# Pooled attention and an affine MLP: two parameter rows made by one product, bias rows written by ScalarE, the mix's rests in one piece

## The chip, the cores and the metric

One core of a Trainium2 chip. The metric is the device time of one execution in microseconds (us). PE is TensorE, PEld its weight loads, DVE VectorE, ACT ScalarE, POOL GpSimd, SP SyncE.

## The reference, cut to what matters

```python
B, H, S, D = 8, 8, 576, 64                       # attention over keys and values averaged by 8 rows
scores = scale * np.matmul(q, k_p.transpose(0, 1, 3, 2))
attn = softmax(scores); x = attn @ v_p           # x: (8, 576, 512)
a1  = alpha1 * x + beta1
tok = np.einsum('ts,bsd->btd', w_tok, a1)        # the "mix" over the 576 tokens
u   = x + lam * tok
a2  = alpha2 * u + beta2
out = u + lam * (np.maximum(a2 @ w_ch1, 0.0) @ w_ch2)
```

The kernel folds lambda into the mix's operand: it needs the row lambda alpha1 broadcast to 128 partitions, and the row lambda beta1 as one extra row of the operand, once for each of its two operand buffers. A "rest" below is the part of an operand that holds the last 64 of the 576 tokens, which four tiles of 128 leave over.

## The kernel before

The opening of the program, in program order for each engine:

```python
vecs = const.tile([65, 3, DM], FP, ...)          # lambda, alpha1, beta1; rows 0 and 64
ones_row = const.tile([1, P], FP, ...)
nc.vector.memset(ones_row, 1.0)
warm = const.tile([P, DM], BF, ...)              # filled by four memsets, used by nothing
...
nc.scalar.dma_start(out=vecs[0:65:64, 0], in_=moe_lam.unsqueeze(0).to_broadcast((2, DM)))
nc.scalar.dma_start(out=vecs[0:1, 1], in_=moe_alpha1.unsqueeze(0))
nc.scalar.dma_start(out=vecs[0:65:64, 2], in_=moe_beta1.unsqueeze(0).to_broadcast((2, DM)))
load_qk(0, 0)                                    # bulk loads on SyncE's queue
load_rem(0)
...
nc.vector.tensor_tensor(out=vecs[0:1, 1], in0=vecs[0:1, 1], in1=vecs[0:1, 0], op=ALU.mult)

def broadcast(i):                                # PE: a row to 128 partitions
    ps = psB.tile([P, DM], FP, tag="ch", bufs=2, name="ps_bc")
    nc.tensor.matmul(out=ps, lhsT=ones_row, rhs=vecs[0:1, i])
    return ps

def row_of_xs(i, eng):                           # lambda beta1, a product on one partition
    p0 = 64 - 64 * i
    eng.tensor_tensor(out=xs_pool[i][p0:p0 + 1, 4, :], in0=vecs[p0:p0 + 1, 2],
                      in1=vecs[p0:p0 + 1, 0], op=ALU.mult)
...
row_of_xs(0, nc.gpsimd)
fill_mix()                                       # GpSimd memsets
ps_lam = broadcast(0)
nc.scalar.copy(out=lam_bc, in_=ps_lam)
ps_lamal = broadcast(1)
nc.scalar.copy(out=lamal_bc, in_=ps_lamal)
cast_q(0, 0, nc.vector.tensor_copy)              # queries to bf16
att_F(0, 0)                                      # PE turns the queries
sum_k(0, 0, nc.vector)                           # pooled keys
fill_E()                                         # 12 VectorE memsets
cast_rem(0, nc.gpsimd)                           # the last 64 tokens' queries and keys
...
att_K(0, 0, nc.vector.tensor_copy, nc.scalar.copy)
...
# first batch of the MLP, among 16 first-product groups:
todo.append((13.0, lambda: row_of_xs(1, nc.gpsimd)))
```

The softmax here doesn't subtract the row's maximum and nothing guards it: scores larger than these inputs give would overflow.

## Time and profile before

| | before |
|---|---|
| median of 3 runs | 368.66 us (367.91 to 369.07) |
| span of the profiled run | 366.2 us |
| busy PE, DVE, ACT, POOL | 97%, 58%, 59%, 35% |
| first exponential (ACT) starts | 11.33 us |
| first mix matmul starts | 24.59 us |
| second product (PE, the output matmuls) starts | 50.47 us |
| from there to the end | 315.72 us |

The span falls into an opening up to the first mix matmul, the first batch up to the second product, and the rest, in which PE is the bound.

### The profile page before, as it was taken

What the parts mean: (1) busy time and instruction counts of PE and PEld (TensorE: products, weight loads), DVE (VectorE), ACT (ScalarE), POOL (GpSimd) and SP (SyncE); (2) the same over time, 40 slices, a digit from 0 to 9 for tenths busy, and PEclk for the clock granted to TensorE, in tenths of its full rate; (3) what the DMA queues carried; (4) which work ended last, traced back from release to release, by engine and by line L of the source; (5) the groups of instructions that cost most, each with busy time, mean ns of one, the idle gap of its engine ahead of it and who ended that gap; (6) DMA issues with size and microseconds to landing.
All of it is one profiled execution on the core that took longest, in us unless ns stands there. A gap on an engine that the chain in (4) does not pass through costs nothing.

```text
span 366.2 us, 6166 instructions
## 1 busy us (share of the span) xinstructions
PE 353.7 (97%) x2340; PEld 192.9 (53%) x2340; DVE 212.9 (58%) x431; ACT 216.1 (59%) x425; POOL 126.4 (35%) x181
## 2 busy tenths in 40 slices
PE   5799999999999999999999999999999999999995
PEld 2367655455545554555455554555455545544543
DVE  7774635883785268724864387627862787543011
ACT  3866993379627960798169924895279615803800
POOL 8856913081509140543245130905090500000000
PEclk9989999999999999999999999999999999999999
DMA  7999994039014910182108311470100002002012
GB/s 249 269 228 319 248 289 128 29 127 345 31 39 147 291 28 33 57 310 79 59 36 307 104 44 44 159 259 29 59 29 2 30 30 58 2 29 86 2 45 71
DMA packets 19552, 43.28 MB, mean 118 GB/s; under 512 B 2169, under 2 KB 4541, under 8 KB 19522
## 3 DMA queue, kind: packets, MB, share of 16 engines
q1 hardware_dynamic: 17496, 37.89, 30.4%
q0 software_dynamic: 1856, 4.86, 7.0%
q8 instruction: 18, 0.29, 0.3%
q10 hardware_dynamic: 170, 0.14, 0.2%
q14 instruction: 12, 0.10, 0.1%
HBM read 38.30 MB, written 9.44 MB: 130 GB/s over the span
## 4 chain that ended last, share of the span: by engine, by line
PE 88%; ACT 6%; DVE 2%; DMA 1%; POOL 1%; issue 0%; ACTq 0%; POOLq 0%
PE ps_ch L587 33%; PE ps_h L564 32%; PE ps_tok L517 9%; PE ps_sc L454 4%; PE ps_av L471 2%; PE ps_uT L548 2%; ACT Hj L569 2%; PE ps_q L370 2%; DMA vecs<-in_moe_beta_dram 1%; PE ps_tok L533 1%; ACT ET L456 1%; ACT qT L374 1%; PE ps_av L474 1%; ACT wtT L292 0%; ACT vp L445 0%
## 5 line engine op out<-in xcount | busy, mean ns | idle before, releaser
L564 PE MATMUL ps_h<-u_fm,w 128*128 128x512 bf16 (+1 forms) x592 | 134.7, 373 | 0.7 <-ACT u_fm L550 0.4
L587 PE MATMUL ps_ch<-w,Hj 128*128 128x512 bf16 x512 | 127.2, 379 | 0.0
L569 ACT ACTIVATE Hj<-ps_h,bias_cols 128x512 bf16<-128x512 f32 x144 | 97.1, 691 | 33.9 <-PE ps_h L564 33.4
L564 PEld LDWEIGHTS <-w 128*128 128x128 bf16 x592 | 63.9, 114 | 48.6 <-issue 0.9
L587 PEld LDWEIGHTS <-Hj 128*128 128x128 bf16 x592 | 55.5, 98 | 49.4 <-issue 0.7
L550 ACT COPY u_fm<-ps_uT 128x512 bf16<-128x512 bf16 x36 | 21.1, 588 | 70.1 <-PE ps_uT L548 70.0
L485 POOL TENSOR_TENSOR xs<-x_tm,lamal_bc 128x512 bf16<-128x512 f32 x24 | 30.5, 1270 | 82.2 <-DVE x_tm L478 81.9
L456 ACT ACTIVATE ET<-ps_sc 128x288 f16<-128x288 f32 (+1 forms) x128 | 51.5, 489 | 10.6 <-PE ps_sc L454 10.3
L594 DVE TENSOR_TENSOR u_sb<-u_sb,ps_ch 128x512 f32<-128x512 f32 (+1 forms) x37 | 24.9, 672 | 24.9 <-PE ps_ch L587 23.8
L517 PE MATMUL ps_tok<-xs,wtT 128*128 128x512 bf16 (+1 forms) x160 | 39.3, 379 | 0.0
L409 DVE CAST kpT<-ps_kp 64x288 bf16<-64x288 f32 x30 | 13.6, 455 | 43.5 <-PE ps_kp L405 43.3
L593 DVE TENSOR_TENSOR ps_ch<-lam_bc,ps_ch 128x512 f32<-128x512 f32 x32 | 22.2, 693 | 25.5 <-PE ps_ch L587 25.4
L478 DVE TENSOR_TENSOR x_tm<-ps_av,rec 128x320 f32<-128x320 f32 x64 | 31.5, 492 | 2.8
L476 DVE RECIPROCAL rec<-ps_av 128x5 f32<-128x5 f32 x64 | 12.3, 193 | 35.2 <-PE ps_av L474 35.2
L138 POOL TENSOR_TENSOR qk_raw<-qk_raw 128x512 f32<-128x512 f32 (+1 forms) x28 | 30.1, 1076 | 1.1
L454 PE MATMUL ps_sc<-qT,kpT 128*128 128x288 bf16 (+1 forms) x128 | 29.0, 300 | 1.0 <-DVE kpT L409 0.5
L519 DVE TENSOR_TENSOR u_sb<-x_tm,ps_tok 128x512 f32<-128x512 f32 x32 | 21.9, 685 | 10.0 <-PE ps_tok L517 9.8
L694 POOL COPY ticks<-ticks 1x1 f32<-1x1 f32 x6 | 1.1, 178 | 70.5 <-DVE ticks L690 70.5
L517 PEld LDWEIGHTS <-wtT 128*128 128x128 bf16 (+1 forms) x160 | 15.1, 98 | 18.7 <-DVE xs L485 1.9
L471 PEld LDWEIGHTS <-ET 72*128 72x128 f16 (+1 forms) x256 | 16.8, 101 | 14.7 <-DVE vp L429 0.7
L417 DVE TENSOR_TENSOR v_u<-v_u 128x512 f32<-128x512 f32 (+1 forms) x30 | 22.2, 741 | 0.8
L520 DVE TENSOR_TENSOR u_bf<-u_sb,al_bc 128x512 bf16<-128x512 f32 x31 | 21.8, 704 | 1.1
(117 smaller groups left out, 335.7 us busy)
## 6 DMA issues: line engine op xcount, KB each, us to landing
qk_raw<-in_q_dram SPq DMA_DIRECT2D x16, 512.0 KB, 5.1
qk_raw<-in_k_dram SPq DMA_DIRECT2D x16, 512.0 KB, 7.5
v_u<-in_v_dram SPq DMA_DIRECT2D x32, 256.0 KB, 8.0
out_dram<-u_sb SPq DMA_DIRECT2D x32, 256.0 KB, 2.3
w<-in_moe_w_ch_dram POOLq DMA_DIRECT2D x2, 1024.0 KB, 12.9
w<-in_moe_w_ch_dram POOLq DMA_DIRECT2D x4, 512.0 KB, 10.8
rem_raw<-in_q_dram SPq DMA_DIRECT2D x8, 128.0 KB, 8.9
rem_raw<-in_k_dram SPq DMA_DIRECT2D x8, 128.0 KB, 4.7
```

Of the source, the lines that this page charges most:

```text
L138: eng.tensor_tensor(out=t[:, :, 0:n], in0=t[:, :, 0:n], in1=t[:, :, n:2 * n], op=ALU.add)
L417: eng.tensor_tensor(out=t[:, :, 0:n], in0=t[:, :, 0:n], in1=t[:, :, n:2 * n], op=ALU.add)
L454: nc.tensor.matmul(out=ps_sc[0:n, 0:288], lhsT=kpT_pool[u][:, j, r, 72 * hh:72 * hh + n], rhs=st["qT"][u][:, h % 4, :])
L456: nc.scalar.activation(out=ET[0:n, 64 + j:64 + S + j:2], in_=ps_sc[0:n, 0:288], func=AF.Exp, bias=0.0, scale=1.0 / 64)
L471: nc.tensor.matmul(out=av[:, c, :], lhsT=ET[:, m0:m0 + 256:2], rhs=vp1)
L478: nc.vector.tensor_tensor(out=x[:, :, dd:dd + D], in0=av[:, :, 0:64], in1=rec.unsqueeze(2).to_broadcast((P, 5, D)), op=ALU.mult)
L485: eng.tensor_tensor(out=xs[:, 0:4, cols], in0=x[:, 0:4, cols], in1=lamal_bc[:, cols].unsqueeze(1).to_broadcast((P, 4, D * (h1 - h0))), op= ...
L517: nc.tensor.matmul(out=ps_tok, lhsT=wtT[0:kk, at, P * c:P * c + P], rhs=xs[0:kk, sc, :], start=(sc == 0), stop=(sc == 4))
L564: nc.tensor.matmul(out=ps_h[:, t0:t1], lhsT=w1_of(cc, j), rhs=u_fm[n][:, cc, t0:t1], start=(cc == 0), stop=(cc == 3))
L569: nc.scalar.activation(out=t, in_=ps_h, func=AF.Relu, bias=bias_cols[:, j:j + 1], scale=1.0)
L587: nc.tensor.matmul(out=ps, lhsT=Hj[n, j][:, 128 * m:128 * m + 128], rhs=w2_of(n, j, cols), start=(j == 0), stop=(j == NJ - 1))
L594: nc.vector.tensor_tensor(out=u, in0=u, in1=ps, op=ALU.add)
```

## The change

Its intent is to take a slow one-partition product off GpSimd in the opening. Alpha1 and beta1 are put on two neighbouring partitions, so that one VectorE product makes both lambda rows; a selector matrix lets PE broadcast the second row; ScalarE only copies the bias row. In the first batch the rests of the mix's operand (64 rows) are made in one GpSimd instruction for six heads. Unused warm-up fills go.

```diff
-    vecs = const.tile([65, 3, DM], FP, tag="vecs", name="vecs")
-    ones_row = ...; nc.vector.memset(ones_row, 1.0); warm = ... (4 memsets)
+    vecs = const.tile([2, 2, DM], FP, tag="vecs", name="vecs")
+    prods = const.tile([2, DM], FP, tag="prods", name="prods")
+    pick = const.tile([2, 2, P], FP, tag="pick", name="pick")
+    nc.vector.memset(pick, 1.0)
+    nc.vector.memset(pick[0:1, 1], 0.0)
...
-    nc.scalar.dma_start(out=vecs[0:65:64, 0], in_=moe_lam.unsqueeze(0).to_broadcast((2, DM)))
-    nc.scalar.dma_start(out=vecs[0:1, 1], in_=moe_alpha1.unsqueeze(0))
-    nc.scalar.dma_start(out=vecs[0:65:64, 2], in_=moe_beta1.unsqueeze(0).to_broadcast((2, DM)))
+    nc.scalar.dma_start(out=vecs[:, 0], in_=moe_lam.unsqueeze(0).to_broadcast((2, DM)))
+    nc.scalar.dma_start(out=vecs[0:1, 1], in_=moe_beta1.unsqueeze(0))
+    nc.scalar.dma_start(out=vecs[1:2, 1], in_=moe_alpha1.unsqueeze(0))
...
-    nc.vector.tensor_tensor(out=vecs[0:1, 1], in0=vecs[0:1, 1], in1=vecs[0:1, 0], op=ALU.mult)
+    nc.vector.tensor_tensor(out=prods, in0=vecs[:, 1], in1=vecs[:, 0], op=ALU.mult)
...
-        eng.tensor_tensor(out=xs_pool[i][p0:p0 + 1, 4, :], in0=vecs[p0:p0 + 1, 2], ...)
+        nc.scalar.copy(out=xs_pool[i][p0:p0 + 1, 4, :], in_=prods[0:1])
...
-    row_of_xs(0, nc.gpsimd)
     fill_mix()
     ps_lam = broadcast(0)
     nc.scalar.copy(out=lam_bc, in_=ps_lam)
+    row_of_xs(0)
     ps_lamal = broadcast(1)
...
-    att_X(0, 0, 2, nc.gpsimd)              # and the same for heads 2 to 4
+    att_X(0, 0, 2, nc.gpsimd, False)       # False: without the rests
...
+    att_X_rem(0, 0, 6, nc.gpsimd)
-    att_X_rem(0, 4, 8, nc.vector)
+    att_X_rem(0, 6, 8, nc.vector)
...
-            todo.append((13.0, lambda: row_of_xs(1, nc.gpsimd)))
+            todo.append((13.0, lambda: row_of_xs(1)))
```

## The prediction

> **What bounds the kernel now.** I read the page first (engine shares, the 40 slices, the chain that ended last), then the chain in order of time over the first 60 us, then the timeline of the first 45 us, and last ScalarE between 40 and 51 us, because the change touches only the opening and the first batch.
>
> ```profile
> PE   5799999999999999999999999999999999999995
> ...
> PE 88%; ACT 6%; DVE 2%; DMA 1%; POOL 1%; issue 0%; ACTq 0%; POOLq 0%
> ```
>
> The kernel is TensorE-bound: from slice 3 on PE is at 90% or more, and 88% of the chain is PE. Nothing in the change takes a matmul out of that stretch. So only what moves the moment at which PE gets into its steady work, near 50 us, can move the end, one for one.
>
> ```profile
> 2.20 3.92 DMA vecs<-in_moe_beta_dram
> ...
> 6.26 1.26 POOL xs L274
> 7.53 0.05 issue
> 7.58 0.42 POOL wtT L255
> 8.00 0.46 POOL xs L256
> ...
> 9.58 0.47 POOL rem_k L124
> 10.05 0.05 issue
> 10.10 0.22 PE ps_kp L405
> 10.34 0.46 DVE kpT L409
> ```
>
> Columns are start, length, what. The opening's chain runs through the third small load (beta1, landing about 6.1), then GpSimd's row product (1.26 us for one partition), two fills, the casts of the remainder rows, and so to the keys. This is what the change attacks.
>
> ```profile
> 4.71 0.65 DVE L263 TENSOR_TENSOR vecs<-vecs 1x512 f32<-1x512 f32 x1
> 4.94 1.17 POOL L252 MEMSET ones_lo<- 64x128 bf16 x1
> 5.29 0.67 DVE L130 CAST q_bf<-qk_raw 128x1024 bf16<-128x1024 f32 x1
> 5.42 2.07 PE L268 MATMUL ps_bc<-vecs,ones_row 1*128 1x512 f32 x2 [0.62 <-DVE vecs L263]
> 6.61 1.92 DVE L138 TENSOR_TENSOR qk_raw<-qk_raw 128x512 f32<-128x512 f32 x2 [0.64 <-DMA qk_raw<-in_k_dram]
> 7.42 1.03 PE L370 MATMUL ps_q<-identity_bf,q_bf 128*128 128x128 bf16 x8
> 8.49 1.01 ACT L374 COPY qT<-ps_q 128x1024 bf16<-128x1024 bf16 x1 [0.38 <-PE ps_q L370]
> 8.56 0.63 DVE L139 TENSOR_TENSOR k_bf<-qk_raw 128x256 bf16<-128x256 f32 x1
> 9.40 0.27 ACT L391 COPY qT<-ps_qr 128x128 bf16<-128x128 bf16 x1
> 10.82 0.40 ACT L409 CAST kpT<-ps_kp 64x288 bf16<-64x288 f32 x1 [1.16 <-DVE kpT L409]
> ```
>
> These are the neighbours of that chain. VectorE makes the lambda alpha1 row at 4.71, PE broadcasts it for 2.07 us, and only then turns the queries. The queries are ready at 9.67, 1.15 us before ScalarE's key copy at 10.82: that is all the slack on the query side. From 10.82 to about 20 ScalarE is nearly full (4.88 of 5 us busy between 15 and 20), so what delays it at 11 us delays everything.
>
> **What the Trainium skill says.** "DMA: Bandwidth & Descriptors", section "Queues, rings and completion order": each DMA engine goes round its queues and drains a whole packet of descriptors from one before it turns to the next. The trace agrees: ScalarE's queue moved its data only at about 2.2, 4.1 and 5.4 us (lambda, alpha1, beta1), with bulk loads of q and k between, although alpha1 and beta1 were issued 0.3 us apart (1.90 and 2.20). "SBUF — State Buffer", section "SBUF: two separate sides": VectorE and GpSimd share a port pair as an exclusive lock, which a VectorE instruction with two SBUF inputs or in a two-port mode takes. The trace agrees: the 64-partition fill at 4.94 took 1.17 us under VectorE's product and cast, where its twin just before took 0.20; and VectorE's first key sum at 6.61 took 1.46 us (the longest in its group) beside GpSimd's row product. "TensorE: Matmul & The Clock Gate", "Part 1: The HAM clock gate (the "warmup" mystery)": the window that decides on PE's clock runs freely, not from the kernel's start. The trace has such a dip, a granted clock of 0.85 and 0.81 in the stretches 15 to 20 and 20 to 25 us; where it falls may differ from run to run, so a part of a microsecond here is noise.
>
> **The change, part by part.**
>
> Removed from VectorE: the warm-up fills (1.01 us) and the ones row (0.17); added: two small fills for the selector, about 0.3 from the ones row's 0.17. VectorE is about 0.9 us ahead, and GpSimd loses its wait of 0.82 us for the fills before its first mask. But neither is the last arrival: VectorE's next instruction now waits for all three small loads.
>
> Moved, and costly: the product of two rows. Before, it needed lambda and alpha1, and ran at 4.71. Now it needs lambda, beta1 and alpha1, and alpha1 is issued third. If the third load keeps its place in the round, it lands near 6.0 (beta1 did at about 6.1). The product then runs 6.10 to 6.75 (0.65 us; two partitions cost what one does), the broadcast 6.80 to 8.87 (2.07), the query transposes 8.85 to 9.9 (1.03), ScalarE's query copy 9.95 to 10.86, the rest's copy to 11.13, and the key copy follows at 11.13 in place of 10.82. That is +0.3 us on ScalarE.
>
> Removed from GpSimd: the row product, 1.26 us. The remainder cast then starts when its data are in, about 7 us, so the key remainder is ready near 8.6 in place of 10.05. Key side on VectorE: cast 6.72 to 7.39, sums 1.35 to 2.25 us by the rows above with and without the port lock, so about 9.15, as before (9.19); 12 small fills of together 0.93; the key copy could start at 10.1, but PE's order puts the key matmuls behind the late query transposes: about 10.4. So GpSimd's 1.26 us are mostly not collected; they leave the chain, and the chain goes through alpha1, VectorE's product and PE's broadcast instead.
>
> Added to ScalarE: the bias row, one partition of 512. The cheapest analogue is its 512-wide copy, 0.59 us. In the opening it lies in the broadcast's 2.07 us and costs nothing. In the first batch it comes after an activation that starts at 47.81:
>
> ```profile
> 47.81 0.69 ACT L569 ACTIVATE Hj<-ps_h,bias_cols 128x512 bf16<-128x512 f32 x1
> 48.40 0.52 ACT L429 CAST vp<-ps_v 64x128 f16<-64x128 f32 x2
> 48.94 0.83 ACT L456 ACTIVATE ET<-ps_sc 72x288 f16<-72x288 f32 x2
> ```
>
> No idle time is shown ahead of any of these, and the chain runs through ScalarE from 46.32 to 50.35. So it adds about 0.5 to 0.6 us there, of which I count 0.4 to 0.5, as PE may take up a little. GpSimd's product at 44.07, which goes, was followed by idle time (GpSimd was busy 0.34 of the 5 us after 45): nothing to win.
>
> Rests in one go: GpSimd loses two 64x128 pieces (0.46 and 0.45 us) and gets one of 64x384, an estimate of 0.95 from 1.27 for 512 columns; VectorE's 0.41 for 256 columns falls to about 0.25. It is as much work, later. The mix at 24.59 waits for ScalarE's row sums, and reads the rests in its last of five matmuls, 0.8 us later. Zero.
>
> Sum: +0.3 + 0 + 0.45 = +0.75 us, near 369.4. A quarter of a chance for the early landing below takes 0.3 off: 369.1 us.
>
> **The rivals.** First: alpha1 lands early, near 4.8, since it is one descriptor and its issue shorter than beta1's (0.27 against 0.50 us). Then the product ends near 5.5, the broadcast near 7.6, the keys (VectorE no longer locked by GpSimd's product) near 8.3, and ScalarE's key copy comes near 10.0: the opening gains 0.8 to 0.9, and with the later 0.45 lost the kernel takes about 368.2. For it: GpSimd's product is gone from a proven chain. Against: beta1's late packet, in the same third place. Second: ScalarE's added copy is absorbed, because PE has its own work queued from 46 us; then 369.0 with the late landing, 367.8 with the early one. Against it: PE's group of 48.97 starts right behind ScalarE's value copies (48.40 and 0.52), whose buffer it seems to wait for. Third: the later rests hold up the mix through the port lock, if GpSimd's 0.95 us and VectorE's last two pieces queue up one behind the other; that would end near 25.1, still before the fifth matmul at 25.4; a further slip would cost up to 0.5 us, 369.9.
>
> **Range and chances.** The three runs spread from 367.91 to 369.07, so noise is some 0.6 us to either side; the mechanisms span 367.8 to 369.9. A range of 367.7 to 370.2 should hold it 8 times in 10. Two per cent is 7.4 us, many times anything that the opening can give or take: faster 0.01, within 0.98, slower 0.01.
>
> **What would show it.** In the changed profile: the opening's chain starts at the alpha1 load and goes through VectorE's product, PE's broadcast and the query transposes, not through GpSimd; the product starts near 6.1, the second broadcast near 6.8, the first exponential near 11.6 (11.33 before). In the first batch a copy of about 0.55 us stands on ScalarE between an activation and the value copies, with the exponential after it later by as much. I am wrong if the product starts before 5.5, if the opening's first exponential comes before 11.0, or if PE's first group of the second product (50.47 before) starts no later than before.

## The result, and the profile after

The changed kernel took 368.49 us (median of 5, 367.95 to 369.41), the kernel before 368.33 us (median of 5) in the same set. The ratio is 1.0005, 95% interval 0.9983 to 1.0027: the same. A ratio here is the mean time of one kernel's fast runs over that of the other's of the same rounds, so not quite the ratio of the medians. The profiled run of the changed kernel, 369.41 us, was the slowest of its five, and that matters for reading it.

Queue issues and instructions of the opening, kernel before (timeline; start, length, engine, what):

```profile
0.74 1.12 ACTq L166 DMA_DIRECT2D vecs<-in_moe_lam_dram  x1
...
1.90 0.27 ACTq L167 DMA_DIRECT2D vecs<-in_moe_alpha_dram  x1
...
2.20 0.50 ACTq L168 DMA_DIRECT2D vecs<-in_moe_beta_dram  x1
...
11.33 1.59 ACT L456 ACTIVATE ET<-ps_sc 72x288 f16<-72x288 f32 x4
...
24.59 3.41 PE L517 MATMUL ps_tok<-xs,wtT 128*128 128x512 bf16 x15
...
50.47 1.02 PE L587 MATMUL ps_ch<-w,Hj 128*128 128x512 bf16 x4
```

The same of the changed kernel:

```profile
0.75 0.53 ACTq L160 DMA_DIRECT2D vecs<-in_moe_lam_dram  x1
...
1.31 0.24 ACTq L161 DMA_DIRECT2D vecs<-in_moe_beta_dram  x1
...
1.58 0.43 ACTq L162 DMA_DIRECT2D vecs<-in_moe_alpha_dram  x1
...
4.60 0.68 DVE L257 TENSOR_TENSOR prods<-vecs 2x512 f32<-2x512 f32 x1 [0.54 <-DMA vecs<-in_moe_alpha_dram]
...
5.33 2.07 PE L263 MATMUL ps_bc<-prods,pick 2*128 2x512 f32 x2 [1.02 <-DVE prods L257]
...
7.67 1.35 DVE L132 TENSOR_TENSOR qk_raw<-qk_raw 128x512 f32<-128x512 f32 x2 [1.79 <-DMA qk_raw<-in_k_dram]
...
11.39 1.58 ACT L452 ACTIVATE ET<-ps_sc 72x288 f16<-72x288 f32 x4
...
25.59 3.41 PE L513 MATMUL ps_tok<-xs,wtT 128*128 128x512 bf16 x14
...
51.97 1.02 PE L583 MATMUL ps_ch<-w,Hj 128*128 128x512 bf16 x4
```

The third small load did not land near 6.0: the product that waits for it starts at 4.60. The two issues before it took less time (lambda 0.53 in place of 1.12 us), so all three had left the queue by 2.0 us in place of 2.7. By the DMA records of ScalarE's queue (read in narrow windows), the third load's data moved at 3.9 us in place of 5.4, and the second's at 3.5 in place of 4.1. Yet the first exponential comes no earlier, because in this run VectorE waited 1.79 us for the first keys, which landed at 7.67 and not at 6.61. From the first key sum to the first exponential it is 3.72 us, before 4.72: that piece did get shorter.

The chain of the changed kernel, in order of time, then runs through another bulk load, and GpSimd behind it:

```profile
4.73 8.72 DMA rem_v_raw<-in_v_dram
13.46 0.07 issue
13.53 0.97 POOL rem_v_raw L431
...
19.45 0.47 POOL v_sum L415
...
25.75 0.22 PE ps_tok L513
```

And PE's granted clock in the five microseconds from 20 on is lower than before. The rows give the stretch, then busy time and count of PE, PEld, DVE, ACT, POOL, then the clock, the DMA share and GB/s; first the kernel before:

```profile
20.00:25.00 5.00, 4.31 (x60) 3.88 (x59) 4.03 (x12) 4.02 (x10) 3.64 (x5) 0.81 1.12 212
```

then the changed one:

```profile
20.00:25.00 5.00, 5.00 (x57) 4.80 (x56) 3.97 (x12) 3.54 (x8) 4.88 (x4) 0.50 1.12 211
```

The mix starts at 25.59 in place of 24.59. In the first batch ScalarE's new copy stands where the prediction put it:

```profile
48.81 0.69 ACT L565 ACTIVATE Hj<-ps_h,bias_cols 128x512 bf16<-128x512 f32 x1
49.39 0.60 ACT L271 CAST xs<-prods 1x512 bf16<-1x512 f32 x1
49.90 0.52 ACT L425 CAST vp<-ps_v 64x128 f16<-64x128 f32 x2
50.44 0.83 ACT L452 ACTIVATE ET<-ps_sc 72x288 f16<-72x288 f32 x2
```

From the activation's start to the exponential's it is 1.63 us here and was 1.13 before (47.81 to 48.94). From the first mix matmul to the second product it is 26.38 us against 25.88: 0.50 more. From there to the end 315.66 against 315.72.

So the trace has two questions in it. Is the 0.50 us real in the end? And is the late opening the change's doing, or chance?

### The profile page after: what moved, and what is told of

Same layout as the page of the kernel before. It is cut to its first block, busy times and chain, and to the rows that moved or that the text cites. A ratio compares the mean times of both kernels' runs of the same rounds, so it can differ in the third digit from the quotient of the medians.

```text
span 367.6 us, 6117 instructions
## 1 busy us (share of the span) xinstructions
PE 352.3 (96%) x2298; PEld 194.2 (53%) x2340; DVE 210.6 (57%) x428; ACT 217.1 (59%) x427; POOL 124.9 (34%) x178
## 4 chain that ended last, share of the span: by engine, by line
PE 86%; ACT 6%; DMA 2%; POOL 2%; DVE 1%; issue 1%; SPq 1%; ACTq 0%; POOLq 0%
PE ps_ch L583 33%; PE ps_h L560 30%; PE ps_tok L513 9%; PE ps_sc L450 4%; ACT Hj L565 3%; DMA rem_v_raw<-in_v_dram 2%; PE ps_uT L544 2%; PE ps_av L467 2%; PE ps_q L366 1%; PE ps_tok L529 1%; ACT qT L370 1%; SPq L78 1%; PE ps_w L285 1%; POOL v_u L413 1%; PE ps_av L470 1%
## 5 line engine op out<-in xcount | busy, mean ns | idle before, releaser
L583 PE MATMUL ps_ch<-w,Hj 128*128 128x512 bf16 x495 | 124.0, 379 | 1.2 <-issue 0.3
L452 ACT ACTIVATE ET<-ps_sc 128x288 f16<-128x288 f32 (+1 forms) x128 | 51.2, 487 | 10.7 <-PE ps_sc L450 10.5
L515 DVE TENSOR_TENSOR u_sb<-x_tm,ps_tok 128x512 f32<-128x512 f32 x32 | 21.9, 684 | 10.1 <-PE ps_tok L513 9.6
L413 DVE TENSOR_TENSOR v_u<-v_u 128x512 f32<-128x512 f32 (+1 forms) x30 | 21.2, 707 | 0.8
## 6 DMA issues: line engine op xcount, KB each, us to landing
w<-in_moe_w_ch_dram POOLq DMA_DIRECT2D x2, 1024.0 KB, 12.5
w<-in_moe_w_ch_dram POOLq DMA_DIRECT2D x4, 512.0 KB, 10.8
```

Of the source, the lines that this page charges most:

```text
L413: eng.tensor_tensor(out=t[:, :, 0:n], in0=t[:, :, 0:n], in1=t[:, :, n:2 * n], op=ALU.add)
L452: nc.scalar.activation(out=ET[0:n, 64 + j:64 + S + j:2], in_=ps_sc[0:n, 0:288], func=AF.Exp, bias=0.0, scale=1.0 / 64)
L583: nc.tensor.matmul(out=ps, lhsT=Hj[n, j][:, 128 * m:128 * m + 128], rhs=w2_of(n, j, cols), start=(j == 0), stop=(j == NJ - 1))
```

## The experiments

Three theories. One: ScalarE's copy in the first batch lies on the chain and costs all of its 0.50 us. Two: the opening gains something behind the landing of the keys, and what the first trace shows against it (late keys, slow clock) is chance. The rivals: PE absorbs the copy; and the change itself delays the opening. The readings of all traces first, in us. "Product" is VectorE's lambda product, "keys" the start of its first key sum, "exp" the first exponential, "full clock" the time from which PE keeps its full clock up to the mix and beyond, "mix" the first mix matmul, "batch" the stretch from there to the second product.

| run | product | keys | exp | full clock | mix | batch | span | median of the time, ratio to before |
|---|---|---|---|---|---|---|---|---|
| before | 4.71 | 6.61 | 11.33 | 21.9 | 24.59 | 25.88 | 366.19 | 368.33 (the set beside the changed kernel) |
| before_again | 4.87 | 7.15 | 11.49 | 21.3 | 24.49 | 25.86 | 366.00 | 368.48, 0.9992 |
| before_third | 5.07 | 8.21 | 12.04 | 21.5 | 25.21 | 25.87 | 366.80 | 368.47, 0.9999 |
| changed | 4.60 | 7.67 | 11.39 | 25.1 | 25.59 | 26.38 | 367.63 | 368.49, 1.0005 |
| after_again | 5.18 | 6.53 | 10.65 | 21.4 | 24.11 | 26.38 | 366.10 | 368.25, 0.9993 |
| after_third | 4.57 | 7.81 | 11.52 | 22.3 | 24.95 | 26.58 | 367.18 | 368.96, 1.0018 |
| row_early | 4.68 | 6.53 | 10.15 | 22.4 | 23.93 | 25.88 | 365.57 | 367.60, 0.9969 |
| early_again | 4.62 | 7.60 | 11.32 | 23.8 | 25.05 | 25.86 | 366.55 | 368.11, 0.9987 |
| row_pool | 4.71 | 6.68 | 10.24 | 19.3 | 23.01 | 26.40 | 365.12 | 367.68, 0.9971 |
| row_x5 | 4.80 | 7.42 | 11.00 | 21.5 | 24.36 | 29.48 | 370.38 | 372.27, 1.0092 |
| pool_prod | 4.88 | 6.86 | 11.12 | 23.6 | 24.91 | 26.39 | 366.93 | 368.66, 0.9997 |
| alpha_late | 7.63 | 8.92 | 13.18 | 23.3 | 26.26 | 26.38 | 368.26 | 370.44, 1.0051 |
| rests_split | 5.03 | 7.63 | 11.19 | 22.6 | 24.92 | 26.38 | 366.93 | 368.38, 0.9993 |
| cast_first | 5.35 | 7.77 | 11.45 | 21.5 | 24.84 | 26.12 | 366.69 | 368.62, 1.0008 |

The 95% interval of each ratio is about 0.0012 to 0.0016 to either side (0.0022 in the changed kernel's first set). In after_again, pool_prod and alpha_late VectorE came to its key sum straight from other work, so there "keys" is the latest that they can have landed.

### The copy in the first batch: row_early, early_again, row_pool, row_x5

row_early moves the copy to where ScalarE waits for the mix:

```diff
     setup_rowsum(3)
+    row_of_xs(1)
     mix_T(0, 0)
...
-            todo.append((13.0, lambda: row_of_xs(1)))
```

> The changed kernel with the second bias row copied by ScalarE right after the last row sum, where ScalarE waits 3.16 us for PE, instead of in the first batch's full stretch. Theory 1 (the copy sits on the chain and costs its whole 0.50 us there): the stretch from the first mix matmul to the first group of the second product falls from 26.38 us in the changed kernel to 25.9 (25.88 in the kernel before), and the median comes out about 0.5 us lower, near 368.0. Rival (PE absorbs the copy, the 0.50 us of the trace is chance): the stretch stays within 0.1 of 26.38 and the time does not move. On either theory the rest behind that group stays 315.7 us.

ScalarE's lines there, in the timeline of row_early:

```profile
24.47 0.62 ACT L271 CAST xs<-prods 1x512 bf16<-1x512 f32 x1
27.61 0.59 ACT L546 COPY u_fm<-ps_uT 128x512 bf16<-128x512 bf16 x1 [2.52 <-PE ps_uT L544]
```

The copy ends at 25.09 and ScalarE still waits 2.52 us for PE. The batch stretch is 25.88, the kernel before's own value. Theory one holds. The median, 367.60, is 0.4 us lower than expected. The opening of the profiled run was a lucky one (keys at 6.53); the other four left no trace, so why the set as a whole was so fast stays open. The kernel before took 368.48 (before_again). The second set of the same version:

> The version with the second bias row copied in ScalarE's idle time, beside the changed kernel in one call. Theory: 0.5 us or a little more below the changed kernel, 0.6 to 1.2 us below the kernel before (ratio 0.997 to 0.9985). Rival (the first result of 0.9969 was a lucky set): ratio above 0.9985.

368.11 us, ratio 0.9987 with an interval of 0.9972 to 1.0003, beside the changed kernel's 1.0018: 0.85 us better than the changed kernel by the medians. The ratio misses the 0.9985 I had set by a hair, on the rival's side, and the batch stretch is 25.86 again. So the early copy is the better place by both traces and by the times, and this version is the fastest here that was run twice; that it beats the kernel before is clear of noise in one set (0.9957 to 0.9981) and not quite in the other.

row_pool keeps the copy's place, but gives it to GpSimd:

```diff
-            todo.append((13.0, lambda: row_of_xs(1)))
+            todo.append((13.0, lambda: row_of_xs(1, nc.gpsimd.tensor_copy)))
```

> The changed kernel with the second bias row copied by GpSimd at the same place in the program. Theory 1: the stretch from the first mix matmul to the first group of the second product is 25.9 us, as in the kernel before, and ScalarE's exponential follows its activation without the 0.50 us between. Rival: 26.4 as in the changed kernel.

The time agrees (367.68, 0.9971), the stretch does not: 26.40, the rival's number. The chain of waits of row_pool tells why:

```profile
22.82 9.50 DMA rem_raw<-in_k_dram
32.32 0.07 issue
32.39 0.47 POOL rem_raw L117
...
35.51 0.73 POOL k_bf L133
```

And in its timeline PE stood still for GpSimd's key sums:

```profile
36.28 0.29 PE L398 MATMUL ps_kp<-sel_k,k_bf 128*128 128x128 bf16 x2 [0.30 <-POOL k_bf L133]
```

The first batch waited for its load of the next batch's key rests and for GpSimd's key sums behind it. ScalarE's activation and value copies follow each other without the copy (46.75, 47.34, 47.88 in its timeline, 1.13 us as before). So the 0.5 us was lost elsewhere. All traces together show where. In eleven of the fourteen, PE's key matmul of the next batch (ps_kp) starts 12.74 to 12.77 us after the first mix matmul, and GpSimd's key sum (k_bf) has ended by 12.50. In after_third, cast_first and row_pool that sum ends at 12.90, 12.93 and 13.22, and PE's key matmul comes at 12.96, 12.99 and 13.27: 0.2, 0.2 and 0.5 us late. By so much their batch stretches exceed the others' 25.87 (without the copy) or 26.38 (with it; row_x5 apart): 26.58, 26.12 and 26.40. By this reckoning row_pool would have had about 25.9 without its late load, and theory one stands. In each of the three GpSimd waited 1.1 us or more for the rests to land, in the others 0.7 at most. An early mix is not what does it: after_third and cast_first had theirs at 24.95 and 24.84.

row_x5 does the copy five times at the changed kernel's place:

```diff
+            for _ in range(5):
                 todo.append((13.0, lambda: row_of_xs(1)))
```

> The changed kernel with the second bias row copied five times by ScalarE at its place (same result). Theory 1 (one to one on the chain, about 0.50 us for each copy): the stretch from the first mix matmul to the first group of the second product grows from 26.38 by 4 times 0.5 to about 28.4 us, and the time by 2.0 us to about 370.5. Rival (absorbed by work that PE has queued): below 27.0 and below 369.2.

ScalarE in row_x5, and two rows of its stretches (columns as above):

```profile
48.13 3.20 ACT L271 CAST xs<-prods 1x512 bf16<-1x512 f32 x5
```

```profile
48.00:50.00 2.00, 0.52 (x3) 0.16 (x2) 0.00 (x0) 1.94 (x4) 0.00 (x0) 1.00 1.12 239
52.00:54.00 2.00, 2.00 (x12) 1.17 (x11) 0.27 (x2) 2.00 (x6) 0.00 (x0) 0.56 1.04 409
```

It is not absorbed at all; it costs more than one to one. The stretch is 29.48, 3.10 above the changed kernel's for four more copies. Of that, copies in a row take 0.64 us each, so four make about 2.6; PE is busy 0.52 of 2 us at 48 to 50, 0.20 at 50 to 52, and then gets a granted clock of 0.56 at 52 to 54. The slow clock reaches past the second product: its way to the end is 316.54 in place of 315.7, the one exception to my ruler. 372.27 is 3.5 us above the kernel before and 3.8 above the changed kernel's first median, nearly twice the 2.0 expected.

### The opening: before_again, before_third, after_again, after_third

> The kernel before, once more, to see how much of the opening is chance. Theory 2 (the opening of the two kernels differs only by chance: when the bulk loads land and where PE's slow clock falls): the first mix matmul starts anywhere between 24.3 and 25.8 us, and moves with the landing of the value rests (12.58 in the first trace of the kernel before, 13.53 in the changed one). Rival (the change itself delayed the opening by 1.0 us): the first mix matmul within 0.2 of 24.59.

24.49, with the value rests taken up at 12.38: by this run alone the rival, that the change itself delayed the opening, stood as well.

> The changed kernel once more, in one call with the next three. Theory (the change shortens the opening behind the landing of the keys by about 0.9 us and gives 0.5 us back with ScalarE's copy in the first batch): first exponential 3.6 us after VectorE's first key sum (3.72 in its first trace; 4.72 and 4.34 in the two of the kernel before), stretch from the first mix matmul to the second product 26.4 us, and a median 0.3 to 0.6 us below the kernel before. Rival (it changes nothing, 1.0005 was the truth): median within 0.2 us of the kernel before.

From the keys to the first exponential 4.12 us and not 3.6 (see the next part: here the product set it, 5.47 us behind its start); mix at 24.11, 1.5 us earlier than in the same kernel's first trace. That the late opening was the kernel's own doing falls with this. The time, 0.9993, misses the 0.3 to 0.6 us expected and sides with the rival.

> The changed kernel beside the next two in one call. Theory: the median within 0.4 us of the kernel before, since about 0.6 us gained at the first exponential is partly lost to chance further on and 0.5 us is given back in the first batch.

It is 0.45 us above the kernel before by the medians, just more than expected, and the interval of the ratio, 1.0006 to 1.0030, lies above 1: the changed kernel was slower. Its keys came at 7.81, and its batch stretch lost 0.2 us to the next batch's load (see row_pool).

> The kernel before, a third trace. Theory (when the first keys land is chance: 6.53 to 7.81 us in the traces with the changed opening, 6.61 and 7.15 in the two of the kernel before): anywhere between 6.5 and 7.8, with the first exponential at the later of 5.1 us behind GpSimd's product and about 4.4 behind the keys. Rival (the changed order of the small loads holds the keys up): 7.2 or earlier again. The stretch from the first mix matmul to the second product is 25.9 us on either.

8.21 us, the latest landing of all and later than expected, in the kernel before. So early or late keys are no mark of either kernel. The first exponential came 3.83 us behind them, not 4.4, and 5.09 behind GpSimd's product, which started at 6.95. As in the two other traces of this kernel, PE's last wait, 0.45 us, was for GpSimd's key rests.

### What sets the first exponential: alpha_late, pool_prod, cast_first

```diff
-    nc.scalar.dma_start(out=vecs[1:2, 1], in_=moe_alpha1.unsqueeze(0))
...
     load_rem(0)
+    nc.sync.dma_start(out=vecs[1:2, 1], in_=moe_alpha1.unsqueeze(0))
     load_qk(0, 1)
```

> The changed kernel with the alpha1 load issued on the bulk loads' queue behind those of the query and key rests, so that it lands late, as the prediction took it to do. Theory (product, PE's broadcast, query transposes and ScalarE's copies follow each other and set the first exponential): it comes 5.5 us after the start of VectorE's product (10.15 less 4.68 and 10.24 less 4.71 in the traces with early landing), so with a product at 7.0 near 12.5, and the time rises by about 2 us over the changed kernel. Rival (PE and ScalarE have slack there): the first exponential stays below 11.5 and the time within 0.3 us of the changed kernel.

The chain of alpha_late is the one that the prediction drew for a late alpha1:

```profile
7.63 0.76 DVE prods L257
8.40 0.04 issue
8.44 2.07 PE ps_bc L263 x2
10.51 0.98 PE ps_q L366 x8
11.51 1.01 ACT qT L370
12.53 0.18 ACT qT L387
12.74 0.40 PE ps_sc L450
```

The exponential comes at 13.18, 5.55 us after the product's start. The median is 370.44, 2.2 us above after_again. Nothing in that path has slack once the product is late. (The edit also puts the bulk loads behind it on SyncE's queue off by about 0.5 us; the chain does not run through them here.)

```diff
     fill_ones()
+    nc.gpsimd.tensor_tensor(out=xs_pool[0][0:1, 4, :], in0=vecs[0:1, 1],
+                            in1=vecs[0:1, 0], op=ALU.mult)
     fill_mix()
```

> The changed kernel with a product of one partition and 512 columns given back to GpSimd ahead of the fills (into rows that are overwritten later; the result stays right). Theory (GpSimd's product was what held the key remainder): the first exponential comes 4.3 to 4.7 us after VectorE's first key sum again, in place of 3.6, and the time rises by 0.7 to 1.0 us over the changed kernel. Rival (the port lock between the two engines or the key landing sets it, not the product): 3.6 to 3.8 us and no change of time.

From keys to exponential it is 4.26 us, at the edge of the theory's number, but not on its path. The timeline of pool_prod:

```profile
4.53 1.25 POOL L602 TENSOR_TENSOR xs<-vecs 1x512 bf16<-1x512 f32 x1
...
4.88 1.45 DVE L257 TENSOR_TENSOR prods<-vecs 2x512 f32<-2x512 f32 x1 [0.82 <-DMA vecs<-in_moe_alpha_dram]
```

VectorE's product, 0.68 us in the changed kernel, takes 1.45 and ends 0.55 after GpSimd's, as under the port lock that the prediction cites. PE's broadcast follows at 6.38, and so the exponential (11.12, 6.24 after the product's start). From the product's end it is 4.79 us, and it is 4.79 in after_again, row_early and alpha_late too. So GpSimd's product hurt by holding up VectorE here, not by making the key rests late. The run did not rebuild the kernel before, where GpSimd's product came at 6.26 to 6.95, behind VectorE's. The time rose by 0.4 us over after_again by the medians, ratios 0.9997 and 0.9993: half of what I expected, and not clear of noise.

cast_first is row_early with VectorE's query cast ahead of the product, and PE's query transposes ahead of the broadcast:

```diff
-    row_of_xs(0); ps_lamal = broadcast(1); nc.scalar.copy(out=lamal_bc, in_=ps_lamal)
     cast_q(0, 0, nc.vector.tensor_copy)
+    nc.vector.tensor_tensor(out=prods, in0=vecs[:, 1], in1=vecs[:, 0], op=ALU.mult)
     att_F(0, 0)
+    row_of_xs(0); ps_lamal = broadcast(1); nc.scalar.copy(out=lamal_bc, in_=ps_lamal)
```

> As the version with the early copy, but VectorE casts the queries before it makes the two products, and PE turns the queries before it broadcasts. Theory (the first exponential is the later of product start plus 5.5 us and key sum plus 3.6 us): the product no longer sets it, so it comes 3.6 to 3.8 us after the first key sum, and does not follow the alpha1 load; 0 to 0.4 us faster than the version with the early copy. Rival (PE's broadcast, now in front of the key matmuls, delays them instead): over 4.0 us after the first key sum, and no faster.

The exponential came 3.68 us after the first key sum, as the theory says, but keys landed at 7.77 in this run, where the product would not have set it in any order. The time, 368.62, is 0.5 us above early_again: the expected gain did not come. Its batch stretch is 26.12, with the next batch's key rests in the chain as in row_pool; 0.26 us more than in early_again's trace. Whether the new order makes that load late is open.

### The rests: rests_split

```diff
-    att_X(0, 0, 2, nc.gpsimd, False)       # and heads 2 to 4
+    att_X(0, 0, 2, nc.gpsimd)
-    att_X_rem(0, 0, 6, nc.gpsimd)
-    att_X_rem(0, 6, 8, nc.vector)
+    att_X_rem(0, 4, 8, nc.vector)
```

> The changed kernel with the rests of the mix's operand in pieces as in the kernel before. Theory (this part is neutral: the mix waits for ScalarE's and PE's row sums): median within 0.3 us of the changed kernel. Rival (the later rests hold the mix through the port lock, VectorE's last piece took 1.08 us beside GpSimd's 1.54 us in the trace with the early copy): 0.4 us or more faster than the changed kernel.

368.38 beside after_again's 368.25, both at 0.9993: neutral. The merged piece took GpSimd 1.54 us in the changed kernel's trace, and VectorE's last one 1.08 beside it, and in after_again they ended at 24.2 and 24.3, behind the start of the mix at 24.11. The mix did not wait: its first 15 matmuls took 3.41 us there, as in the kernel before.

### What the runs say together

With the product at p and the keys at k, the changed opening's first exponential is at the later of p + 5.5 and k + 3.6 (to 3.7): 10.65 from 5.18, 10.15 from 4.68 (its keys at 6.53 give the same), 11.39 from 7.67, 11.19 from 7.63. Before, it was GpSimd's product (6.26, 6.43, 6.95) plus 5.1 in all three traces. So the change does take GpSimd's product off the path. Against the first trace of the kernel before it gains 0.7 to 1.2 us when the keys land early, and nothing when they land at 7.6 or later. Over the three traces of the kernel before the exponential is at 11.62 on average, over the seven with the changed opening as it stands (changed, after_again, after_third, row_early, early_again, row_pool, row_x5) at 10.90: 0.72 us gained. At the first mix matmul the averages are 24.76 and 24.43: 0.33 us left of it, and less than the scatter (23.01 to 25.59 among the seven). Between the two lies PE's clock. The latest change to full clock (25.1) goes with the latest mix (25.59) and the earliest (19.3) with the earliest (23.01), across one and the same opening. All fourteen traces say the same: the later the full clock comes after the exponential, the longer, by and large, is the way from the exponential to the mix. It is 12.77 us when the clock comes 9.1 us after (row_pool), 13.0 to 13.4 at 9.5 to 10.2, 13.3 to 13.5 at 10.5 to 10.8, 13.7 to 13.8 at 11.4 to 12.5, and 14.20 at 13.7 (changed). So an exponential that comes earlier, while the clock changes when it did, loses part of its gain. This is a relation between traces; no run set the clock by itself.

Then the copy takes 0.50 back. Adding up: -0.33 and +0.50 make +0.2 us; the three measured ratios of the changed kernel, 1.0005, 0.9993 and 1.0018, average 1.0005, which is 0.2 us too. That they agree so well is partly chance: the first of the two terms is not clear of scatter, and the interval of the third ratio begins only at 1.0006.

## Why the prediction was right or wrong

The time, 368.49 against 369.1, lay in the range, and "within 2%" was right. Luck has a part in it: of the two terms of the sum the later one was right (+0.45, measured 0.50), while the opening's +0.3 had the wrong sign (-0.33 on average at the first mix matmul, not clear of scatter), and the range from 367.7 to 370.2 would have held no change at all as well. Of the three signs of being wrong that the prediction names, the first came true in all three traces of the changed kernel (product at 4.60, 5.18 and 4.57, before 5.5), the second in one (exponential at 10.65, before 11.0), the third in none (second product at 51.97, 50.49 and 51.53, not before 50.47). Of the steps:

- The bound, and that only the first 50 us count: right. The way behind the second product was 315.6 to 315.8 us in all traces but the one with five copies.
- ScalarE's copy in the first batch, 0.4 to 0.5 us on the chain: right; 0.50. That PE would take up a little was not so.
- "If the third load keeps its place in the round, it lands near 6.0", from which came a product at 6.10 and +0.3 us: wrong, and the step that failed. The third load landed at 4.55 us in row_early and 5.05 in after_again (by their chains), and the product started at 4.57 to 5.18 (5.35 in cast_first, where it stands behind the cast). In the first trace the third load's data moved at 3.93 us, before at 5.40. About 0.5 of these 1.5 us the second load had already (3.53 for 4.07): lambda, written to neighbouring partitions, took 0.53 us to issue and not 1.12, and the queue was done at 2.02 and not 2.70. The rest is that the third load's data followed the second's by 0.40 us and not by 1.33 (0.40 to 0.76 in all ten traces with alpha1 third on this queue, 1.22 to 1.33 to the first of beta1's two rows in the three of the kernel before). Beta1 went to two rows and alpha1 to one; whether that is the cause I did not test. The rival's reason, alpha1's shorter issue of 0.27 us, is not it: in the third place that issue took 0.43.
- The chain behind the product (broadcast, transposes, copies): right in its durations, and tested with a late alpha1: 5.55 us, where the prediction's 6.10 to an exponential near 11.6 makes 5.5.
- "GpSimd's 1.26 us are mostly not collected": half right. With early keys 0.7 to 1.2 us were collected at the first exponential, with late ones little. This is the first rival, to which I gave a quarter; its "near 10.0" for ScalarE's key copy was met where the keys were early (9.69 to 10.19). Its 368.2 was met by one of the three sets of the changed kernel.
- "It is as much work, later. Zero" for the rests: right, though the merged piece took 1.54 us and not the estimated 0.95.
- VectorE's key sums, "1.35 to 2.25 us by the rows above": not what those rows show, which is 1.92 and 0.63, together 2.58 from 6.61 to 9.19; the changed kernel took 1.97 (7.67 to 9.64).
- The port lock: the prediction's example is read too widely. Beside VectorE's product alone the same fill took 0.20 us (before_again), and the next larger one, 64x512, 0.51 (row_x5); that one took 1.5 to 1.6 only where the cast came as well (four traces). That fits the section it cites, which lets a VectorE instruction with two SBUF inputs block only a GpSimd operation that reads SBUF, a limit the prediction left out; a fill reads nothing. The products in pool_prod both read SBUF.
- Not foreseen: when the first keys land varies by 1.7 us between runs of like kernels (6.53 to 8.21), more than any term of the sum. The range had room for it only because it was cut from the scatter of the times.

## What to carry to other kernels

Before moving work to an idle engine, look at the exact slot: the same 0.6 us copy was free 24 us into the kernel, where ScalarE waited for PE, and cost 0.50 us 25 us later, where the chain ran through ScalarE. Work taken off a chain pays only down to the next arrival, here the landing of the keys or of the parameters. And when a trace shows a microsecond's difference, take a second trace of the same kernel before explaining it: the first one here was the slowest run of five and told of a delay that the kernel did not have.

## What the Trainium skill lacked or had wrong

- "DMA: Bandwidth & Descriptors", "Queues, rings and completion order": the turn-taking fits the small loads of the kernel before, but the section does not tell how far landings scatter: the first key load landed at 6.53 to 8.21 us with the same bulk loads ahead of it.
- No page gives for this chip what an issue on ScalarE's queue costs by the shape of its target: two rows 64 partitions apart took 1.10 to 1.13 us as the first load, two neighbouring rows 0.53 to 0.54.
- "TensorE: Matmul & The Clock Gate", "Part 1: The HAM clock gate (the "warmup" mystery)": a freely running window fits: in the kernel before the granted clock changes at 15.08, 18.49 and 21.91 us, in the changed one at 14.82, 18.23 and 25.06, each step once or twice the page's 3413 ns. But the page's about 3.4 us of sustained activity does not say how much activity suffices. In the kernel before PE was busy 3.22 us of the stretch before 15.08, and the clock went up; 2.19 of the next, and it went down. In early_again it was busy 3.16 of 3.41 us from 16.94 to 20.35, and the clock rose only one such stretch later, at 23.77; in row_pool 3.19 from 15.90 to 19.32 raised it.
